# Storing a fill's inputs as high and low parts, so that the wide tiles of the first MLP load both directly

## The chip, the cores and the metric

The kernel runs on one core of one Trainium2 chip. The metric is the time of one execution on the device, in microseconds (us); lower is better. Engines are named as in the profile: PE (matrix multiply), PEld (its weight loads), DVE (vector), ACT (scalar), POOL (GpSimd), SP (the queue from which every DMA of this kernel is issued; the profile writes SPq for its instructions).

## What is computed

Causal attention with a memory term, then two MLPs one after the other, all in float32:

```python
scores = q @ k.T / 8, causal;  a = softmax(scores);  local = a @ v
mem = (phi(q) @ M_prev) / (phi(q) . z_prev + 1e-6)
x0 = gate * mem + (1 - gate) * local      # 4 batches, 8 heads, 576 positions, 64 wide
x  = x0 as 2304 tokens x 512
x1 = elu(x @ w1_in) @ w1_out              # 512 -> 2048 -> 512
out = leaky(x1 @ w2_in) @ w2_out
```

The weights of the MLPs are float64 in memory and are decoded on the chip.

## The kernel before, in words

**Number format.** A matrix product in full precision is made of three products in the faster rounded format (F32R): a value x is split into a high part xh (x rounded, a cast on ACT) and a low part xl (x minus xh, a subtraction on POOL), a weight likewise, and wh·xh, wl·xh and wh·xl are added up in PSUM (`h_mm`, line 615; `o_mm`, line 642). So each x that goes into an MLP costs a cast and a subtraction before PE can use it.

**Order of the work.** First attention, batch by batch. The first MLP is cut in two over its hidden size. The first 7 of its 16 hidden blocks of 128 (NFA, line 47) are worked off as a **fill** between the attention's pieces (`phase1_units`, line 661): each batch is cut into 2 parts of 288 tokens, 8 parts in all (`parts`, line 152). For a part, `u_x` (line 669) gathers its x (one load from `xm_scr` for batch 0; for the other batches two halves from `xq_scr` that DVE adds, line 682), stores it to `x_scr` for later (line 683; batch 0 has it in `xm_scr` already), and splits it into `xh0/xl0` or `xh1/xl1` (`split_x`, line 607: 4 casts on ACT, 4 subtractions on POOL at line 612). `u_h` and `u_o` make the hidden blocks and a partial output, which is copied to a tile `st` and stored to `y_scr` (line 697).

The other 9 hidden blocks follow in the **wide tiles** (line 822): 5 tiles of 512 tokens (the last has 256). A wide tile's x is read back by `load2` (line 814): for each half of 256 tokens, `recut` (line 786) loads the token ranges of the parts into the one staging tile `x` (one buffer, in a pool of its own), then 4 casts on ACT write the high part into `xw0` or `xw1` and 4 subtractions on POOL (line 806) write the low part into `xv0` or `xv1`. Two sets of buffers take turns, so a tile's x is made while the tile before is multiplied. Each hidden block goes through ACT twice (`elu`, lines 631 and 632), DVE twice (line 633, and the cast to `gh` at 244) and POOL once (`gl`, line 626) before `emit_out` multiplies it on. At a tile's end, DVE adds the stored `y` (line 852) half by half, through two buffers `st`, and the sums are stored to `x1_scr` (line 853). The 9 weight blocks of this part are loaded (lines 102, 106) and decoded beside it: ACT 126, DVE 127, 128, 131, ACT 242 (the cast to w), POOL 137 twice. The second MLP then runs in wide tiles of the same kind, and reads its x through `load3` and the same staging tile.

**What sets the order.** The program's order gives each instruction a priority, shifted by `tc.high_priority`, and a scheduler that simulates the engines' time lays every engine's instructions out in one fixed list; each engine, SP among them, then goes through its list in order and waits where it must. The first wide tile's load stands 150 steps ahead of its place (line 820). The load of tile i+1 stands in the program just ahead of the last `emit_out` of tile i (line 845).

**Memory that is shared.** When the fill ends, its pools are closed and new ones take the same memory (`close_mlp`, line 732); a new tile waits for the old tiles under it alone. By the sizes and the order of first use, `xw0` and `xv0` lie on the fill's `x`, `y`, `xh0` and `xl0`; `xw1` on the end of the old `gl`, on both `st` and on `xh1`; `xv1` on `xh1` and `xl1`; the new `e` on the old `e` and the first `gh`.

Of the kernel before, what the change touches and what calls it, by code (L numbers as in the profile page):

```python
# [8 lines left out]
F32 = mybir.dt.float32  # L9
F32R = mybir.dt.float32r  # L10
# [5 lines left out]
P = 128  # L16
# [3 lines left out]
def _f(ap):  # L20
    return ap.bitcast(F32)
# [3 lines left out]
def kernel(  # L25
# [14 lines left out]
    nc = tc.nc  # L40
# [4 lines left out]
    NKC = DM // P  # L45
# [6 lines left out]
    V32 = 1  # L52
# [7 lines left out]
    TN = 256  # L60
    TW = 512
# [9 lines left out]
    dram = ctx.enter_context(tc.tile_pool(name="dram", bufs=1, space=bass.MemoryType.DRAM))  # L71
# [70 lines left out]
    def tile_tok(t):  # L142
        b, ca, cb = t
        r0 = CH[ca][0]
        r1 = CH[cb - 1][0] + CH[cb - 1][1]
        return b * S + r0, r1 - r0

    def halves(n):
        return [(0, n)] if n <= 320 else [(0, n // 2), (n // 2, n // 2)]


    parts = [(i, o, w, tile_tok(t)[0] + o) for i, t in enumerate(tiles1) for o, w in halves(tile_tok(t)[1])]
    xm_scr = [dram.tile([P, NKC, tile_tok(t)[1]], F32, name=f"xm{i}") for i, t in enumerate(tiles1)]
    xq_scr = [
        [dram.tile([P, NKC, tile_tok(t)[1]], F32, name=f"xq{i}_{j}") for j in range(2)] for i, t in enumerate(tiles1)
    ]
    x_scr = [
        xm_scr[t][:, :, o:o + w] if t < V32 else dram.tile([P, NKC, w], F32, name=f"xs{i}")
        for i, (t, o, w, _) in enumerate(parts)
    ]  # L160
    y_scr = [dram.tile([P, NKC, p[2]], F32, name=f"ys{i}") for i, p in enumerate(parts)]
    x1_scr = [dram.tile([P, NKC, TN], F32, name=f"x1s{i}") for i in range(NTT)]

# [43 lines left out]
    def bank(tag):  # L207
        return psum.tile([P, 512], F32, tag=tag, bufs=BANKS[tag], name=tag)
# [31 lines left out]
    def copy(eng, dst, src):  # L240
        if eng == "A":
            nc.scalar.copy(dst, src)  # L242
        else:
            (nc.vector if eng == "V" else nc.gpsimd).tensor_copy(dst, src)  # L244

    def split(hi, lo, src, full=False):
        if full:
            nc.scalar.copy(_f(hi), src)
            return
        nc.scalar.copy(hi, src)  # L250
        nc.vector.tensor_tensor(out=lo, in0=src, in1=_f(hi), op=ALU.subtract)  # L251
# [350 lines left out]
    def mtile(tag, bufs, dt=F32, shape=None):  # L602
        shape = shape or (NW,)
        pool = pools.get(("own", tag), pools["mlp"])
        return pool.tile([P] + list(shape), dt, tag=tag, bufs=bufs, name=tag)

    def split_x(xt, w, par):
        xh = mtile(f"xh{par}", 1, F32R, (NKC, NW))[:, :, 0:w]
        xl = mtile(f"xl{par}", 1, F32R, (NKC, NW))[:, :, 0:w]
        for c in range(NKC):  # L610
            copy(E_XH, xh[:, c], xt[:, c])
            nc.gpsimd.tensor_tensor(out=xl[:, c], in0=xt[:, c], in1=_f(xh[:, c]), op=ALU.subtract)
        return xh, xl

    def h_mm(ph, wi, xh, xl):
        n_mm = 0
        for kc in range(NKC):
            for wj, xx in ((0, xh), (1, xh), (0, xl)):
                nc.tensor.matmul(ph, wi[:, wj, kc, :], xx[:, kc, :], start=n_mm == 0, stop=n_mm == 11)  # L619
                n_mm += 1  # L620
# [8 lines left out]
    def elu(ph, w):  # L629
        e = mtile("e", EB)[:, 0:w]  # L630
        nc.scalar.activation(out=e, in_=ph, func=AF.Relu, scale=-1.0)
        nc.scalar.activation(out=e, in_=e, func=AF.Exp, scale=-1.0)
        nc.vector.scalar_tensor_tensor(out=e, in0=e, scalar=-1.0, in1=ph, op0=ALU.add, op1=ALU.max)  # L633
        return g_split(e, w)
# [7 lines left out]
    def o_mm(py, fs, key, ec, gs, first, last, opens=True, closes=True):  # L642
        for f in fs:
            wo = wo_tiles[key, f]
            gh, gl = gs[f]
            for n_mm, (wj, gg) in enumerate(((0, gh), (1, gh), (0, gl))):
                nc.tensor.matmul(  # L647
                    py, wo[:, wj, ec * P:(ec + 1) * P], gg,
                    start=opens and f == first and n_mm == 0, stop=closes and f == last and n_mm == 2,
                )  # L650
# [5 lines left out]
    def h_bank():  # L656
        nonlocal n_ph
        n_ph += 1
        return bank("tp" if tail and n_ph % 2 else "pm")

    def phase1_units(ti):

        units = []
        for pi, (pt, o, w, _) in enumerate(parts):
            if pt != ti:
                continue
            st = {}

            def u_x(pi=pi, o=o, w=w, st=st):
                xt = mtile("x", 1, F32, (NKC, NW))[:, :, 0:w]  # L670
                if ti < V32:
                    nc.sync.dma_start(xt, xm_scr[ti][:, :, o:o + w])
                    st["x"] = split_x(xt, w, pi % 2)
                    st["g"] = {}
                    return
                x2 = mtile("y", 1, F32, (NKC, NW))[:, :, 0:w]
                for j in range(2):
                    ps, pz = slice(64 * j, 64 * j + 64), slice(64 - 64 * j, 128 - 64 * j)
                    nc.sync.dma_start(xt[ps], xq_scr[ti][j][ps, :, o:o + w])
                    nc.sync.dma_start(x2[ps], xq_scr[ti][j][pz, :, o:o + w])  # L680
                for c in range(NKC):
                    nc.vector.tensor_tensor(out=xt[:, c], in0=xt[:, c], in1=x2[:, c], op=ALU.add)
                nc.sync.dma_start(x_scr[pi], xt)
                st["x"] = split_x(xt, w, pi % 2)
                st["g"] = {}

            def u_h(f, w=w, st=st):
                ph = h_bank()[:, 0:w]
                h_mm(ph, wi_tiles[0, f], *st["x"])
                st["g"][f] = elu(ph, w)  # L690

            def u_o(ec, pi=pi, w=w, st=st):
                py = bank("sc" if tail else "pm")[:, 0:w]
                o_mm(py, range(NFA), 0, ec, st["g"], 0, NFA - 1)
                y = mtile("st", 2)[:, 0:w]
                copy(E_Y, y, py)
                nc.sync.dma_start(y_scr[pi][:, ec], y)

            units.append((0, u_x))
            for f in range(NFA):  # L700
                units.append((HC * 12 * w / 2.4, lambda f=f, u=u_h: u(f)))
            for ec in range(NKC):
                units.append((3 * NFA * w / 2.4, lambda ec=ec, u=u_o: u(ec)))
        return units
# [48 lines left out]
    for c, u, done in att:  # L753
# [11 lines left out]
        while fill and fill[0][0] <= pos and fill[0][1] <= credit:  # L765
            _, c2, u2 = fill.pop(0)
# [19 lines left out]
    def recut(dst, scr, t0, n):  # L786
        for pi, (_, _, w, tok) in enumerate(parts):
            lo, hi = max(tok, t0), min(tok + w, t0 + n)
            if lo < hi:
                nc.sync.dma_start(dst[:, :, lo - t0:hi - t0], scr[pi][:, :, lo - tok:hi - tok])  # L790

    n_wide = 0

    def load_x(fetch, t0, n):

        nonlocal n_wide
        par = n_wide % 2
        n_wide += 1
        xh = mtile(f"xw{par}", 1, F32R, (NKC, TW))[:, :, 0:n]
        xl = mtile(f"xv{par}", 1, F32R, (NKC, TW))[:, :, 0:n]  # L800
        for o in range(0, n, TN):
            xt = mtile("x", 1, F32, (NKC, TN))
            fetch(xt, t0 + o)
            for c in range(NKC):
                copy(E_XH, xh[:, c, o:o + TN], xt[:, c])
                nc.gpsimd.tensor_tensor(  # L806
                    out=xl[:, c, o:o + TN], in0=xt[:, c], in1=_f(xh)[:, c, o:o + TN], op=ALU.subtract
                )
        return xh, xl
# [2 lines left out]
    wide = [(t0, min(TW, NT - t0)) for t0 in range(0, NT, TW)]  # L812

    def load2(t0, n):
        return load_x(lambda xt, t: recut(xt, x_scr, t, TN), t0, n)

    def load3(t0, n):
        return load_x(lambda xt, t: nc.sync.dma_start(xt, x1_scr[t // TN]), t0, n)

    with tc.high_priority(offset=EARLY):  # L820
        cur = load2(*wide[0])
    for gi, (t0, w) in enumerate(wide):
# [21 lines left out]
        if gi + 1 < len(wide):  # L844
            cur = load2(*wide[gi + 1])
# [14 lines left out]
    for gi, (t0, w) in enumerate(wide):  # L860
# [25 lines left out]
        for tb in range(w // P):  # L886
            r0 = t0 + tb * P
            for hf in range(2):
                cs = slice(hf * DM // 2, (hf + 1) * DM // 2)
                o = mtile("st", 2, F32, (DM // 2,))  # L890
# [32 lines left out]
```

## Time and profile before

| what | value |
|---|---|
| median of 3 runs | 1110.76 us (1110.44 to 1112.65) |
| the profiled execution's own time | 1110.38 us |
| its span, first to last instruction | 1108.6 us |
| mean granted clock of PE, as a share of full speed | 0.989 |
| busy: PE | 1062.3 us (96%) |
| busy: PEld | 916.4 us (83%) |
| busy: DVE | 600.1 us (54%) |
| busy: ACT | 493.6 us (45%) |
| busy: POOL | 563.7 us (51%) |
| DMA | 104.43 MB, mean 94 GB/s |

A view by stretches gives each engine's busy time in a stretch, with the granted clock of PE; a timeline lists an engine's instructions in order of time, with the idle time before one in square brackets and the engine or transfer whose end released it; a view of groups sums the instructions of one line. Idle time of an engine other than PE costs nothing by itself. Times in the timelines count from the span's start. Attention and the fill reach to about 470, the first MLP's wide tiles lie at about 453 to 712, and the second MLP is at about 697 to the end.

### The profile page before, as it was taken

Reading aid. Unit: us, or ns where it says so; the run is one execution under the profiler, and the core shown is the slowest. Engines: PE = TensorE matmul, PEld = TensorE weight load, DVE = VectorE, ACT = ScalarE, POOL = GpSimd, SP = SyncE. Lnnn points to the kernel's source line nnn. Section 1 sums busy time; section 2 is a strip of 40 time slices with the busy share of each in tenths; the row PEclk is TensorE's granted clock in tenths of the full one; section 3 lists DMA queues with packets and bytes.
Section 4 is the critical chain, followed back from the end, with each engine's and each line's share of the span. In section 5 each row is a group of like instructions: output and inputs, shape, how many; then the busy total and the mean of one; then the engine's idle time right before and its main releaser. Section 6 shows DMA issues by size and latency. Waiting matters only on the chain.

```text
span 1108.6 us, 17441 instructions
## 1 busy us (share of the span) xinstructions
PE 1062.3 (96%) x5904; PEld 916.4 (83%) x5904; DVE 600.1 (54%) x1398; ACT 493.6 (45%) x1205; POOL 563.7 (51%) x710
## 2 busy tenths in 40 slices
PE   6998899999989998979999999999999999999997
PEld 3877799989979998967777889888888888888896
DVE  6889978787869837656565223655222232132232
ACT  5898878687858635444343223432111111111110
POOL 7676785775747527666575224855322322222222
PEclk9999999999999999989999999999999999999999
DMA  7654533744462147543635113431200100010010
GB/s 180 186 144 96 135 89 92 174 112 116 109 171 80 51 150 225 158 140 124 201 115 168 56 40 96 152 114 38 67 10 1 48 29 1 1 39 1 1 38 20
DMA packets 145912, 104.43 MB, mean 94 GB/s; under 512 B 81440, under 2 KB 139808, under 8 KB 145824
## 3 DMA queue, kind: packets, MB, share of 16 engines
q1 hardware_dynamic: 145824, 103.33, 32.4%
q8 instruction: 47, 0.77, 0.3%
q14 instruction: 41, 0.34, 0.1%
HBM read 73.80 MB, written 25.95 MB: 90 GB/s over the span
## 4 chain that ended last, share of the span: by engine, by line
PE 69%; DMA 8%; DVE 8%; POOL 6%; issue 4%; ACT 3%; SPq 2%; DVEq 0%; POOLq 0%; ACTq 0%
PE pm L619 16%; PE sc L871 14%; PE tp L619 12%; PE sc L647 5%; PE po L871 4%; PE po L525 4%; PE pm L647 4%; PE tp L458 3%; POOL xv L806 2%; PE sc L429 2%; POOL w L137 1%; PE po L647 1%; PE sc L430 1%; DMA wraw<-in_moe_w_out_dram 1%; DMA x1s<-st 1%
## 5 line engine op out<-in xcount | busy, mean ns | idle before, releaser
L626 POOL TENSOR_TENSOR gl<-e,gh 128x512 fp32r<-128x512 f32 (+2 forms) x181 | 202.7, 1123 | 358.3 <-DVE gh L244 314.6
L619 PE MATMUL tp<-xw,w 128*128 128x512 f32 (+1 forms) x504 | 147.1, 374 | 5.6 <-DVE e L633 5.6
L619 PE MATMUL pm<-xw,w 128*128 128x512 f32 (+1 forms) x496 | 143.9, 372 | 0.0
L871 PE MATMUL sc<-w,gh 128*128 128x512 f32 x448 | 137.7, 393 | 0.0
L647 PE MATMUL sc<-gh,w 128*128 128x512 f32 (+2 forms) x438 | 108.6, 347 | 5.7 <-DVE st L852 2.9
L619 PEld LDWEIGHTS tp<-xw,w 128*128 128x128 f32 x504 | 92.2, 190 | 24.3 <-DVE e L633 6.0
L452 POOL TENSOR_SCALAR pt<-pt,rs,omg 128x128 f32<-128x128 f32 (+4 forms) x160 | 102.0, 646 | 19.6 <-DVE rs L447 18.1
L619 PEld LDWEIGHTS pm<-xw,w 128*128 128x128 f32 x496 | 90.5, 188 | 18.4
L437 ACT ACTIVATE pt<-pt,mx 128x128 f32<-128x128 f32 (+4 forms) x160 | 93.3, 584 | 24.9 <-DVE mx L432 23.4
L871 PEld LDWEIGHTS sc<-w,gh 128*128 128x128 f32 x448 | 83.1, 188 | 17.9
L619 PE MATMUL tp<-xv,w 128*128 128x512 f32 (+1 forms) x252 | 94.1, 374 | 0.0
L619 PE MATMUL pm<-xv,w 128*128 128x512 f32 (+1 forms) x248 | 92.0, 371 | 0.0
L647 PEld LDWEIGHTS sc<-gh,w 128*128 128x128 f32 x438 | 75.6, 190 | 17.7 <-issue 3.8
L638 ACT ACTIVATE e<-pm 128x512 f32<-128x512 f32 (+1 forms) x40 | 22.2, 555 | 151.6 <-PE pm L619 151.6
L619 PE MATMUL pm<-xh,w 128*128 128x288 f32 x368 | 82.1, 309 | 5.9 <-DVE e L633 4.5
L244 DVE CAST gh<-e 128x512 fp32r<-128x512 f32 (+2 forms) x146 | 76.2, 524 | 20.6 <-PE po L647 8.0
L458 PE MATMUL tp<-ident,pt 128*128 128x128 f32 x480 | 81.7, 276 | 5.4 <-DVE dl L251 2.0
L871 PE MATMUL sc<-w,gl 128*128 128x512 f32 x224 | 85.4, 393 | 0.0
L639 DVE TENSOR_TENSOR e<-tp,e 128x512 f32<-128x512 f32 (+1 forms) x40 | 25.5, 636 | 107.7 <-ACT e L638 107.6
L639 DVE TENSOR_TENSOR e<-pm,e 128x512 f32<-128x512 f32 (+1 forms) x40 | 25.5, 637 | 106.9 <-ACT e L638 106.9
L137 POOL TENSOR_TENSOR w<-wm,w 128x512 fp32r<-128x512 f32 x50 | 66.2, 1343 | 30.1 <-ACT w L242 30.1
L638 ACT ACTIVATE e<-tp 128x512 f32<-128x512 f32 (+1 forms) x40 | 22.1, 553 | 117.4 <-PE tp L619 117.2
(155 smaller groups left out, 2509.1 us busy)
## 6 DMA issues: line engine op xcount, KB each, us to landing
wraw<-in_moe_w_in_dram SPq DMA_DIRECT2D x32, 512.0 KB, 4.1
wraw<-in_moe_w_out_dram SPq DMA_DIRECT2D x32, 512.0 KB, 4.9
ys<-st SPq DMA_DIRECT2D x32, 144.0 KB, 3.1
x1s<-st SPq DMA_DIRECT2D x36, 128.0 KB, 1.8
x<-x1s SPq DMA_DIRECT2D x9, 512.0 KB, 3.7
out_dram<-st SPq DMA_DIRECT2D x36, 128.0 KB, 1.7
vn<-in_v_dram SPq DMA_DIRECT2D x64, 64.0 KB, 2.4
xq<-xp SPq DMA_DIRECT2D x24, 160.0 KB, 2.0
```

The lines of the kernel that those rows point to most:

```text
L137: nc.gpsimd.tensor_tensor(out=w[:, 1, a], in0=t[:, a], in1=_f(w)[:, 0, a], op=ALU.subtract)
L244: (nc.vector if eng == "V" else nc.gpsimd).tensor_copy(dst, src)
L437: nc.scalar.activation(out=pt[0:m, 0:nk], in_=pt[0:m, 0:nk], func=AF.Exp, scale=-1.0, bias=mx[0:m, last:last + 1], accum_out=self.pd["ss"] ...
L452: nc.gpsimd.tensor_scalar(out=pt, in0=pt, scalar1=rs[0:m, i:i + 1], scalar2=omg[0:m, h:h + 1], op0=ALU.mult, op1=ALU.mult,)
L458: nc.tensor.transpose(dst, self.p[c][:, k0:k0 + kn], ident)
L525: nc.tensor.matmul(po[:, a:b], w, x, start=i == 0, stop=i == len(mms) - 1)
L619: nc.tensor.matmul(ph, wi[:, wj, kc, :], xx[:, kc, :], start=n_mm == 0, stop=n_mm == 11)
L626: nc.gpsimd.tensor_tensor(out=gl, in0=g, in1=_f(gh), op=ALU.subtract)
L638: nc.scalar.mul(t, ph, 0.01)
L639: nc.vector.tensor_tensor(out=t, in0=ph, in1=t, op=ALU.max)
L647: nc.tensor.matmul(py, wo[:, wj, ec * P:(ec + 1) * P], gg, start=opens and f == first and n_mm == 0, stop=closes and f == last and n_mm == 2,)
L871: nc.tensor.matmul(pos[tb], gg[:, tb * P:(tb + 1) * P], wo[:, wj, :], start=f == 0 and n_mm == 0, stop=f == NF - 1 and n_mm == 2,)
```

## The change

The fill stores the high and the low part of each part's x (`xp_scr`, 16 buffers in DRAM) instead of x; for batch 0, which had no store of its own, too. `load2` loads both parts straight into `xw` and `xv`, the whole tile's width at a time, without the staging tile, the casts and the subtractions. `load3` is as it was.

```diff
-    x_scr = [
-        xm_scr[t][:, :, o:o + w] if t < V32 else dram.tile([P, NKC, w], F32, name=f"xs{i}")
-        for i, (t, o, w, _) in enumerate(parts)
-    ]
+    xp_scr = [[dram.tile([P, NKC, p[2]], F32, name=f"x{n}{i}") for i, p in enumerate(parts)] for n in "hl"]
...
             def u_x(pi=pi, o=o, w=w, st=st):
+                def split():
+                    st["x"] = split_x(xt, w, pi % 2)
+                    for n in range(2):
+                        nc.sync.dma_start(xp_scr[n][pi], _f(st["x"][n]))
+                    st["g"] = {}
+
                 xt = mtile("x", 1, F32, (NKC, NW))[:, :, 0:w]
                 if ti < V32:
                     nc.sync.dma_start(xt, xm_scr[ti][:, :, o:o + w])
-                    st["x"] = split_x(xt, w, pi % 2)
-                    st["g"] = {}
+                    split()
                     return
...
-                nc.sync.dma_start(x_scr[pi], xt)
-                st["x"] = split_x(xt, w, pi % 2)
-                st["g"] = {}
+                split()
...
-    def load_x(fetch, t0, n):
-
+    def wide_x():
         nonlocal n_wide
         par = n_wide % 2
         n_wide += 1
-        xh = mtile(f"xw{par}", 1, F32R, (NKC, TW))[:, :, 0:n]
-        xl = mtile(f"xv{par}", 1, F32R, (NKC, TW))[:, :, 0:n]
+        return [mtile(f"{nm}{par}", 1, F32R, (NKC, TW)) for nm in ("xw", "xv")]
+
+    def load_x(fetch, t0, n):
+
+        xh, xl = (x[:, :, 0:n] for x in wide_x())
...
     def load2(t0, n):
-        return load_x(lambda xt, t: recut(xt, x_scr, t, TN), t0, n)
+        xs = wide_x()
+        for x, scr in zip(xs, xp_scr):
+            recut(_f(x), scr, t0, n)
+        return [x[:, :, 0:n] for x in xs]
```

## Rows read from the trace of the kernel before

**Rows 1.** Busy time by stretch: start:end, length, each engine's busy us (instructions), PEclk, DMA.
```profile
428.00:440.00 12.00, 10.14 (x74) 9.67 (x73) 10.36 (x11) 3.71 (x6) 9.95 (x8) 1.00 0.39 140
...
472.00:484.00 12.00, 6.40 (x17) 4.74 (x16) 6.24 (x8) 5.71 (x12) 8.14 (x8) 0.72 0.62 188
...
600.00:700.00 100.00, 100.00 (x520) 84.44 (x519) 30.87 (x62) 29.24 (x60) 36.11 (x37) 1.00 0.22 64
```

**Rows 2.** Timeline of PE: start, us, line, operation, what ended the idle time before it.
```profile
441.83 0.53 PE L647 MATMUL sc<-gh,w 128*128 128x288 f32 x2 [0.86 <-ACT st L242]
...
478.40 1.22 PE L619 MATMUL tp<-xw,w 128*128 128x512 f32 x2 [5.60 <-DVE e L633]
...
483.69 1.67 PE L647 MATMUL sc<-gh,w 128*128 128x512 f32 x6
...
541.61 0.91 PE L647 MATMUL sc<-gh,w 128*128 128x512 f32 x2 [2.37 <-DVE st L852]
...
545.30 0.66 PE L647 MATMUL sc<-gh,w 128*128 128x512 f32 x2
```

**Rows 3.** The chain that ended last, one undisturbed hidden block of a wide tile.
```profile
616.54 2.80 PE tp L619 x12
```

**Rows 4.** Timeline of ACT around 440 and 472.
```profile
440.16 1.33 ACT L242 CAST xw<-x 128x256 fp32r<-128x256 f32 x4 [5.17 <-POOL xl L612]
...
471.05 1.05 ACT L242 CAST w<-wm 128x1024 fp32r<-128x1024 f32 x1 [1.31 <-DVE wm L131]
472.01 0.58 ACT L631 ACTIVATE e<-tp 128x512 f32<-128x512 f32 x1
...
475.77 1.32 ACT L242 CAST xw<-x 128x256 fp32r<-128x256 f32 x4 [2.69 <-DMA ys<-st]
477.00 0.62 ACT L632 ACTIVATE e<-e 128x512 f32<-128x512 f32 x1
477.54 1.12 ACT L126 ACTIVATE wm<-wraw 128x1024 f32<-128x1024 f32 x1
```

**Rows 5.** Timeline of DVE, the same place.
```profile
477.66 0.69 DVE L633 SCALAR_TENSOR_TENSOR e<-e,tp 128x512 f32<-128x512 f32 x1 [6.64 <-ACT e L632]
```

**Rows 6.** Timeline of POOL.
```profile
440.65 2.80 POOL L806 TENSOR_TENSOR xv<-x,xw 128x256 fp32r<-128x256 f32 x4 [0.52 <-ACT xw L242]
...
472.18 2.49 POOL L137 TENSOR_TENSOR w<-wm,w 128x512 fp32r<-128x512 f32 x2 [5.58 <-ACT w L242]
```

**Rows 7.** Matrix products of the first wide tile that read xw, up to the stall.
```profile
452.00:472.80 20.80, 10.21 (x32) 1.00 0.51 152
```

**Rows 8.** Timeline of SP's queue: the first tile's load, the fill's last stores, a tile boundary.
```profile
443.47 1.21 SPq L790 DMA_DIRECT2D x<-xm  x2
...
471.52 0.46 SPq L697 DMA_DIRECT2D ys<-st  x1
...
523.89 1.20 SPq L790 DMA_DIRECT2D x<-xs  x2
...
525.79 0.51 SPq L106 DMA_DIRECT2D wraw<-in_moe_w_out_dram  x1
527.14 8.67 SPq L853 DMA_DIRECT2D x1s<-st  x4
```

**Rows 9.** The stores of x1 (line 853), from issue to landing.
```profile
DMA to landing us min/median/max: 1.7/1.8/5.9
```

**Rows 10.** Groups of the tiles xw, xv and xl: duration min/median/max in ns.
```profile
L242 ACT CAST xw<-x x72: 391/402/409, 440.2 to 961.7; 128x256 fp32r<-128x256 f32 x72
L806 POOL TENSOR_TENSOR xv<-x,xw x72: 722/739/1733, 440.6 to 963.4; 128x256 fp32r<-128x256 f32 x72
L612 POOL TENSOR_TENSOR xl<-x,xh x32: 789/812/1789, 121.4 to 438.3; 128x288 fp32r<-128x288 f32 x32
```

**Rows 11.** DMA issues: count, KB each, median us to landing.
```profile
xs<-x SPq DMA_DIRECT2D x6, 576.0 KB, 3.5
...
x<-x1s SPq DMA_DIRECT2D x9, 512.0 KB, 3.7
```

## The prediction, made before the change was run

> **What bounds the kernel now.** I read the busy time by stretches first, to see where PE rests. Inside the first MLP's wide tiles it does not: from 600 to 700 it is busy for 100 of 100 us at full clock [rows 1]. There the casts, the subtractions and the staging tile are hidden, and taking them away is worth nothing. What is left to gain lies where the fill ends and the wide tiles begin: from 428 to 440 PE is busy for 10.14 of 12 us, from 472 to 484 for 6.40 of 12, and in the latter the granted clock is 0.72 [rows 1]. The timeline of PE then gives the single waits: 0.86 us at 441.83 for ACT, 5.60 us at 478.40 for DVE, and 2.37 us at 541.61 for DVE's additions at the end of the first wide tile [rows 2].
>
> The large one is followed back through the timelines. PE waits at 478.40 for DVE's step of line 633 at 477.66 [rows 5], which waited 6.64 us for ACT's second step (line 632) at 477.00. ACT had done the first step (line 631) at 472.01, so this second step could have followed within a microsecond or so. But ACT goes through its list in order, and between them stand four casts to xw for the second wide tile, which sat until 475.77 and ended what they waited for with the landing of the last store of y from st [rows 4, 8]. The reason is in the code: xw1 lies on the fill's st. The casts' data is not needed for tens of microseconds; their wait for the buffer blocks work that PE needs at once. The same happens at 440.16, where four casts to xw0 hold ACT for 5.17 us until the last part's subtraction has read x [rows 4], and PE's 0.86 us is for a copy of ACT behind them.
>
> After its long rest PE also runs slowly: the 12 products from 478.40 to 483.69 take 5.29 us where an undisturbed block takes 2.80 [rows 2, 3], 2.5 us lost. At 541.61 the 9 products up to 545.30 take 3.69 us, against 2.10 (9/12 of 2.80), 1.6 us lost [rows 2, 3].
>
> **The change, part by part.**
>
> Removed from the wide tiles: 36 of the 72 casts to xw, at 0.40 us 14.5 us of ACT, and 36 of the 72 subtractions to xv, at 0.74 us 26.6 us of POOL [rows 10]. As engine time this is worth nothing where PE is full. What counts is the two places where the casts block.
>
> At 472: without the casts ACT goes from line 631 to line 632 at about 473.1 (two first steps of 0.58 us from 472.01), not 477.00. That alone starts PE 3.9 us sooner, at 474.5, with 1.7 us of rest left. POOL loses four subtractions of 2.80 us at 440.65 and four more at 450 [rows 6], both ahead of the weight chain whose cast at 471.05 stands ahead of ACT's step at 472.01 [rows 4]; that chain should run 2 to 4 us earlier, which takes most of the rest away too. I take 5.0 of the 5.60 us and the 2.5 us of slow clock: **-7.5**. Bounds: -3.9, if the weight chain is no earlier and the short rest still slows the clock, and -8.1, all of it.
>
> At 441: the 0.86 us goes with the casts: **-0.9**. Bounds 0 and -2.7, the latter with the 1.86 us that PE rests between 428 and 440 [rows 1], because x is also free for the next part without waiting for its store (3.5 us to land, rows 11).
>
> At 541: the additions of the first wide tile wait for their two buffers st, whose stores take 5.9 us to land at worst where the median is 1.8 [rows 9]. Ahead of those stores at 527.14 stood 1 MB of x, issued at 523.89, and weights at 525.79 [rows 8]. After the change the next tile's x no longer passes through one staging tile; it can leave as soon as PE has read xw0 for the last time, at about 514 (the casts that needed xw0 ran at about 517), and should be over before the stores begin. The weights stay. Bounds 0 and -4.0 (2.37 + 1.6); I take **-1.5**, nearer to zero since two of the three transfers stay.
>
> Added in the fill: 16 stores of 576 KB in place of 6, which land in about 3.5 us and which nobody waits for soon [rows 11]. Their cost is in SP's queue: the store of the low part waits for POOL's four subtractions, which run 4 x 0.81 = 3.2 us behind the casts [rows 10], and behind it in SP's list are the attention's loads of q, k and v, the copies of kk and the stores of xq. At worst 8 x 3.2 = 26 us of SP would be lost, of which PE would see little, since those loads are issued well ahead. The scheduler puts a store where it thinks it ready, so a wait is the difference between its model and the chip. I take **+1.0**, between -1 (x is free sooner, and 6 stores of x are gone) and +7.
>
> Added for the first wide tile: its x was partly in the staging tile before the fill's buffers came free; now 2 MB in 4 loads can leave only at about 440.1, behind the last part's stores. Half a MB takes 3.7 us [rows 11], so the four quarters take at most 14.8 us one after the other, and the tile would be there between 448 and 455, where the old way has it after four more casts behind the load at 443.47 [rows 8]: about 454. What covers a delay: by 472.8 PE had done 32 of the xw products [rows 7] and half as many with xv, 48 or four blocks, 11.2 us at 2.80; the other 8 us or so of that stretch are the fill's, and can go ahead of them. **+0.5**, between 0 and +4.
>
> For the other tiles, 24 loads in place of 16, each tile's 2 MB 20 us or more ahead of its use: nothing, but for the second rival. The sum is -7.5 - 0.9 - 1.5 + 1.0 + 0.5 = **-8.4 us**. The profiled execution took 1110.38 us, so 1102.0; the median of the runs stands 0.4 above it: **1102.4 us**.
>
> **The rivals.**
>
> *The wait only changes hands.* When the casts are gone, the next instruction in ACT's list may be line 126 of the weight decoding, at 477.54 now [rows 4]. It needs POOL's subtractions of the weights, which end at 472.18 + 2.49 = 474.7 [rows 6]. Placed ahead of line 632 it would run from 474.7 to 475.8, and PE would start at 477.3: 1.2 us won, the clock low as before, and the 1.5 us of added costs against it. That gives about 1110.5. For it: the scheduler mixes the two chains everywhere. Against it: line 632 stands ahead of line 126 now.
>
> *SP's queue takes the wait over, slower than before.* First the row: what ACT waited for at 440.16 and 475.77 was memory to come free, and that need stays [rows 4]. The Trainium skill, "DMA: Bandwidth & Descriptors", section "Anatomy of one DMA", states that a DMA's semaphore wait is done by the issuing sequencer before dispatch; by that rule the wait for xw moves from ACT to SP and holds all DMAs behind it. No row here prices it for these loads. As a mechanism of this kernel: at each of the four boundaries between wide tiles, 2 MB stand in SP's list ahead of the y loads and the x1 stores. If they leave late, those stores land in 5.9 us or more at every boundary [rows 9], and each costs PE what the first costs now, 2.37 + 1.6 = 4.0 us. Three more of them are +12.0, and the -1.5 falls away: -7.5 - 0.9 + 1.5 + 12.0 = +5.1, that is 1115.9 us. It decides at about 520, 7 us (2 MB at twice the rate of a single load) ahead of the stores at 527.14: earlier, it costs nothing. For it: one such case is in the trace. Against it: PE is done with the old buffer some 13 us before the stores.
>
> A whole new list for every engine comes with any change here, and the attention before 428 can shift by a few us either way; that widens the range, and I have no row that says which way.
>
> **How the numbers follow.** Chances: the forecast 0.65, the wait that changes hands 0.15, SP's queue 0.20. The forecast's own range is 1097 to 1107 (its bounds of -15 and of about -3, cut where several would have to come together). The range for 8 in 10 is 1097 to 1114: it takes in the first rival and reaches most of the way to the second. A measurement of this kernel can tell about 0.2% from no change, 2.2 us. Faster by more than that: the forecast nearly whole and a little of the rest, 0.66. Within it: 0.13. Slower: 0.21.
>
> **What would show each step.** Right: in the changed profile PE's wait of over 5 us around 472 is gone and the clock of that stretch is near 1.00; ACT's line 632 follows line 631 within 2 us there; no cast to xw before the second MLP; PE's wait for ACT's copy near 441 is gone. At the first boundary the stores of line 853 land in clearly less than 5.9 us. Wrong: PE waits for xw or xv loads at the start of the first wide tile; waits of 2 us for line 852 at several boundaries; longer waits of SP for line 612 with PE waiting for kk or k in the attention; or the same rest at 472 with line 126 or the weight cast in the casts' place.

## The result, and the profile after

The changed kernel took **1098.55 us** (median of 4 runs, 1095.36 to 1102.78), the kernel before 1111.43 us in the runs beside it: a ratio of 0.989, 95% interval 0.9858 to 0.9922, that is 12.9 us less. Timed again with the last experiments it was 1097.81 us against 1111.06 (0.9902, 0.9876 to 0.9927). The forecast was 1102.4 us in a range of 1097 to 1114. Sign and place were right; the gain is one and a half times the 8.4 us of the sum, and its cause, as the experiments show, was told only in part.

The profiled execution took 1098.26 us with a span of 1096.2. First the total busy times of the changed kernel (engine, busy us, share of the span, instructions):

```profile
PE 1057.6 (96%) x5904; PEld 912.7 (83%) x5904; DVE 600.3 (55%) x1398; ACT 484.8 (44%) x1169; POOL 530.6 (48%) x674
```

PE does the same products as before. To see where the 12.4 us of span went, two marks at equal work serve: the attention's last product `po<-dl,vv` and the first MLP's last product `sc<-gl`. In the view of a line, the last two times of a row are the starts of its first and of its last product. Before:

```profile
L525 PE MATMUL po<-dl,vv x96: 276/280/373, 104.6 to 402.5; 128*128 128x256 f32 x96
...
L647 PE MATMUL sc<-gl,w x219: 276/303/628, 382.4 to 706.8; 128*128 128x512 f32 x54, 128*128 128x288 f32 x42, 128*128 128x256 f32 x14
```

After (all lines behind 157 are renumbered: 647 is now 644, 619 is 616, 631 to 633 are 628 to 630, 852 and 853 are 857 and 858, 612 is 609):

```profile
L522 PE MATMUL po<-dl,vv x96: 276/280/415, 104.4 to 404.1; 128*128 128x256 f32 x96
...
L644 PE MATMUL sc<-gl,w x219: 276/298/499, 384.5 to 694.3; 128*128 128x512 f32 x54, 128*128 128x288 f32 x42, 128*128 128x256 f32 x14
```

Up to the first mark the changed kernel is 1.6 us later. Between the marks it needs 290.2 us instead of 304.3: 14.1 us less. From the second mark to the end of the span both need the same, 401.8 and 401.9 us. So the whole gain lies between the end of the attention and the end of the first MLP, as the prediction said, and ahead of it the changed kernel is a little later.

The busy times by stretch of the changed kernel (columns as in [rows 1]; the five busy times are those of PE, PEld, DVE, ACT and POOL):

```profile
428.00:440.00 12.00, 11.57 (x86) 11.11 (x85) 8.78 (x13) 4.67 (x10) 9.32 (x10) 1.00 0.70 215
...
472.00:484.00 12.00, 11.07 (x48) 8.65 (x47) 9.53 (x12) 5.71 (x7) 6.97 (x5) 1.00 0.93 288
536.00:548.00 12.00, 12.00 (x53) 9.66 (x52) 6.40 (x9) 3.08 (x4) 4.96 (x4) 1.00 0.67 215
600.00:700.00 100.00, 99.55 (x535) 84.80 (x533) 35.71 (x68) 31.44 (x63) 40.03 (x40) 1.00 0.27 82
```

From 472 to 484 PE is busy for 11.07 us where it was 6.40, at a granted clock of 1.00 where it was 0.72 [rows 1]. The stretch with the first tile boundary, 536 to 548, has no rest at all; before, it read:

```profile
536.00:548.00 12.00, 9.63 (x35) 7.35 (x35) 6.19 (x12) 3.41 (x4) 3.73 (x3) 0.86 0.70 210
```

From 600 to 700, where PE was full before, nothing was to be had and nothing came. The timeline of PE in the changed kernel (start, us, what ended the idle time before) shows what remains of the waits:

```profile
421.64 0.54 PE L616 MATMUL tp<-xh,w 128*128 128x288 f32 x2 [1.07 <-DVE e L630]
...
473.30 0.73 PE L616 MATMUL tp<-xw,w 128*128 128x512 f32 x2 [0.93 <-DVE e L630]
```

The 5.60 us of [rows 2] are now 0.93, for the same step of DVE. The timeline of ACT shows why:

```profile
468.26 1.14 ACT L126 ACTIVATE wm<-wraw 128x1024 f32<-128x1024 f32 x1 [2.65 <-POOL w L137]
...
469.58 0.61 ACT L628 ACTIVATE e<-tp 128x512 f32<-128x512 f32 x1
...
470.55 1.17 ACT L629 ACTIVATE e<-e 128x512 f32<-128x512 f32 x2
```

Line 629 (the old 632) runs 0.97 us after line 628 (the old 631); before, 5 us and four casts lay between them [rows 4]. Ahead of both stands line 126, the weight decoding, and it waits for POOL's line 137. That line becomes important below.

At the first tile boundary the timeline of SP's queue in the changed kernel reads:

```profile
511.67 1.88 SPq L790 DMA_DIRECT2D xw<-xh  x3
513.59 4.38 SPq L790 DMA_DIRECT2D xv<-xl  x3
...
523.17 5.54 SPq L858 DMA_DIRECT2D x1s<-st  x4
```

The next tile's loads leave 11.5 us ahead of the first four x1 stores, where before 3.3 us lay between them [rows 8]. From issue to landing those four stores took, in the changed kernel from 520 to 530:

```profile
DMA to landing us min/median/max: 1.8/2.3/2.8
```

and in the kernel before, from 524 to 537:

```profile
DMA to landing us min/median/max: 1.7/3.8/5.9
```

What the new stores do to SP is seen in the fill. The waits of SP's queue from 0 to 430 us in the changed kernel (who waited for whom: us in total, times, longest) hold nine rows for the new stores, line 670, of 15.3 us in all. The five largest:

```profile
SPq L670 <- ACT e L628: 4.4, 1, 4.4
...
SPq L670 <- ACT xh L239: 3.2, 1, 3.2
...
SPq L670 <- ACT e L629: 2.2, 1, 2.2
...
SPq L670 <- ACT kk L298: 1.9, 1, 1.9
...
SPq L670 <- POOL xl L609: 1.7, 2, 1.5
```

### The profile page after: what moved, and what is told of

Its sections match the earlier page's. It is cut to its first block, busy times and chain, and to the rows that moved or that the text cites. A ratio compares the mean times of both kernels' runs of the same rounds, so it can differ in the third digit from the quotient of the medians.

```text
span 1096.2 us, 17406 instructions
## 1 busy us (share of the span) xinstructions
PE 1057.6 (96%) x5904; PEld 912.7 (83%) x5904; DVE 600.3 (55%) x1398; ACT 484.8 (44%) x1169; POOL 530.6 (48%) x674
## 4 chain that ended last, share of the span: by engine, by line
PE 73%; DMA 8%; DVE 7%; POOL 3%; ACT 3%; SPq 3%; issue 3%; DVEq 0%; POOLq 0%; ACTq 0%
PE pm L616 17%; PE sc L876 14%; PE tp L616 13%; PE sc L644 8%; PE po L876 4%; PE pm L644 4%; PE po L522 3%; PE tp L455 3%; PE po L644 2%; DMA wraw<-in_moe_w_out_dram 2%; DMA x<-xq 2%; SPq L212 2%; PE sc L426 1%; PE sc L427 1%; PE pm L522 1%
## 5 line engine op out<-in xcount | busy, mean ns | idle before, releaser
L623 POOL TENSOR_TENSOR gl<-e,gh 128x512 fp32r<-128x512 f32 (+2 forms) x181 | 199.8, 1108 | 369.8 <-DVE gh L241 291.9
L644 PE MATMUL sc<-gh,w 128*128 128x512 f32 (+2 forms) x438 | 106.0, 343 | 1.1 <-DVE st L857 0.7
L429 DVE CUSTOM_DVE_ANT_0 pt<-sc,mask 128x128 f32<-128x128 f32 (+4 forms) x160 | 69.4, 446 | 8.6 <-PE sc L427 4.3
```

Of the source, the lines that this page charges most:

```text
L429: nc.vector.tensor_tensor_reduce(out=pt[0:m, k0:k0 + n], in0=sc[0:m, 0:n], in1=mk, op0=ALU.add, op1=ALU.min, scale=-0.125, scalar=mx[0:m, ...
L623: nc.gpsimd.tensor_tensor(out=gl, in0=g, in1=_f(gh), op=ALU.subtract)
L644: nc.tensor.matmul(py, wo[:, wj, ec * P:(ec + 1) * P], gg, start=opens and f == first and n_mm == 0, stop=closes and f == last and n_mm == 2,)
```

## The experiments

Gains below are against the kernel before in runs on the same chip. In the diffs the lines of the kernel that an experiment starts from are those of the changed kernel, unless "before" is said. Two questions are put: which part of the removed work or waits gave the 12.9 us, and what the new stores cost.

**Half of the work back: the casts, or the subtractions.** The first kernel loads the high part through the staging tile and casts it again, the low part directly:

```diff
-        xs = wide_x()
-        for x, scr in zip(xs, xp_scr):
-            recut(_f(x), scr, t0, n)
+        xh, xl = wide_x()
+        recut(_f(xl), xp_scr[1], t0, n)
+        for o in range(0, n, TN):
+            xt = mtile("x", 1, F32, (NKC, TN))
+            recut(xt, xp_scr[0], t0 + o, TN)
+            for c in range(NKC):
+                copy(E_XH, xh[:, c, o:o + TN], xt[:, c])
```

> The changed kernel with the casts alone put back: the wide tiles of the first MLP load the low part directly, but the high part through the staging tile and 36 casts on ACT. Theory (ACT's casts, waiting for a buffer, held back line 629, the second step of elu, at 472): the rest of PE at 472 is back with 4 to 6 us and a low clock after it, and the staging tile may bring back the wait at the first tile boundary; the time is 6 to 11 us above the changed kernel, 1105 to 1110 us. Rival (the 36 subtractions on POOL stood in the way of the weight decoding and of gl, and the casts were harmless): within 2 us of the changed kernel, 1097 to 1101 us, no rest over 2 us at 472.

The second does the same to the low part, with 36 subtractions of a tile of zeros on POOL and no casts:

```diff
+                nc.gpsimd.tensor_tensor(out=xl[:, c, o:o + TN], in0=xt[:, c], in1=zero, op=ALU.subtract)
```

> The changed kernel with POOL's work alone put back: the high part is loaded directly, the low part through the staging tile and 36 subtractions (of a tile of zeros) on POOL. Theory (ACT's casts): no rest over 2.5 us at 472, within 3 us of the changed kernel, 1097 to 1102 us. Rival (POOL's subtractions): 6 us or more above it, 1105 to 1110 us.

With the casts it took 1103.71 us (ratio 0.9925, 0.9894 to 0.9956), with the subtractions 1103.46 us (0.9922, 0.9892 to 0.9951). Against the kernel before (1110.74 us) they keep 7.0 and 7.3 us of the 12.9: by the medians each half gives back between 5 and 6, and neither is the whole. The intervals of these ratios overlap with the changed kernel's, so the sizes are rough. Both times lie between what the two sides of each expectation said, and settle neither. The casts missed what was expected of them: they do wait again for st at 475, for 0.99 us, but the rest of PE at 472 does not come back. PE's longest wait from 440 to 600 is elsewhere, in the timeline of PE in the kernel with the casts:

```profile
450.11 0.58 PE L644 MATMUL sc<-gh,w 128*128 128x288 f32 x2 [1.74 <-ACT st L239]
```

It is the wait that stood at 441 before, and longer: in ACT's list the casts to xw sit again until the fill's last subtraction has read x, and the copy to st stands behind them (timeline of ACT):

```profile
446.59 1.33 ACT L239 CAST xw<-x 128x256 fp32r<-128x256 f32 x4 [5.24 <-POOL xl L609]
```

In the kernel with the subtractions a rest is at its old place, shorter, in the timeline of PE:

```profile
477.38 0.74 PE L616 MATMUL tp<-xw,w 128*128 128x512 f32 x2 [2.15 <-DVE e L630]
```

and here no cast can be its cause, for there is none. The timeline of ACT has the weight cast between the two steps, waiting for the decoding:

```profile
475.03 1.05 ACT L239 CAST w<-wm 128x1024 fp32r<-128x1024 f32 x1 [2.01 <-DVE wm L131]
475.98 1.15 ACT L629 ACTIVATE e<-e 128x512 f32<-128x512 f32 x2
```

So PE's rest can come by way of the weight decoding alone, with no buffer waited for by a cast. Between the two marks the kernel with the casts needs 294.4 us and the one with the subtractions 301.3, against 290.2 and 304.3 above. That looks like the larger share for the subtractions, but it is one execution each, and the latter was the slowest of its six.

**The wait away, the work kept.** Two kernels leave the kernel before as it is and only place the wide tiles differently in memory: in their traces every engine has the same instructions in the same order as before. In the first, the order in which xw and xv get their memory is swapped, so that xv1 and not xw1 lies on the fill's st:

```diff
-        xh = mtile(f"xw{par}", 1, F32R, (NKC, TW))[:, :, 0:n]
         xl = mtile(f"xv{par}", 1, F32R, (NKC, TW))[:, :, 0:n]
+        xh = mtile(f"xw{par}", 1, F32R, (NKC, TW))[:, :, 0:n]
```

> The kernel before with nothing taken away: only the order in which xw and xv get their memory is swapped, so that xv1 and no longer xw1 lies on the fill's st, and xv0 on x. The casts keep their place and their 0.40 us each, but no longer wait for the last store of y; POOL's subtractions do. Theory (it is the casts' waiting, not their work, that cost the time): no cast to xw waits for a store from st at 472, the rest of PE there shrinks from 5.6 to under 3 us, and the time is 3 to 8 us below the kernel before, 1103 to 1108 us. Rival (the casts' own 14.5 us on ACT, or the work on POOL): within 2 us of the kernel before, 1109 to 1113 us.

The second allocates xw1 and xv1 before the first wide tile, so that neither lies on st:

```diff
+    for nm in ("xw1", "xv1"):
+        mtile(nm, 1, F32R, (NKC, TW))
     with tc.high_priority(offset=EARLY):
         cur = load2(*wide[0])
```

> The kernel before with nothing taken away: xw1 and xv1 get their memory first, so that both lie on the fill's e and gh (free when the fill's last product has run, at about 468.6) and no longer on st (free when its last store has landed, at about 474.7). The attention's lists stay as they were. Theory (what cost the time is a wait for that store in a queue that goes in order, ACT's before, POOL's when the two were swapped): no cast to xw and no subtraction waits for a store of y at 472, PE's rest there falls from 5.6 us to under 2.5 without a new wait for gl, and the time is 4 to 8 us below the kernel before, 1103 to 1107 us. Rival (as with the swap, another wait takes its place, and the work itself must go): within 2 us of the kernel before.

The swap took 1111.4 us (0.9999, 0.9975 to 1.0024), the earlier allocation 1110.04 us (0.9993, 0.9973 to 1.0013): no gain from either, where 3 to 8 and 4 to 8 us were expected; the rival held both times. And yet the wait that the prediction put first is gone. In the swapped kernel the casts follow line 631 at once (timeline of ACT):

```profile
472.30 1.32 ACT L242 CAST xw<-x 128x256 fp32r<-128x256 f32 x4
473.51 0.64 ACT L632 ACTIVATE e<-e 128x512 f32<-128x512 f32 x1
```

and PE's rest is 2.86 us instead of 5.60. Then POOL is late with what PE needs next. The timeline of POOL in the swapped kernel:

```profile
475.05 4.70 POOL L806 TENSOR_TENSOR xv<-x,xw 128x256 fp32r<-128x256 f32 x4 [1.04 <-DMA ys<-st]
479.71 3.52 POOL L626 TENSOR_TENSOR gl<-e,gh 128x512 fp32r<-128x512 f32 x2
```

and in its timeline of PE the new waits for gl:

```profile
474.92 0.73 PE L619 MATMUL tp<-xw,w 128*128 128x512 f32 x2 [2.86 <-DVE e L633]
...
489.77 0.96 PE L647 MATMUL sc<-gl,w 128*128 128x512 f32 x3 [2.35 <-POOL gl L626]
```

From 400 to 720 us PE waits 6.5 us for gl there, in the kernel before 1.4, and its waits in that stretch add up to 15.0 us against 13.3. In the kernel with the earlier allocation no buffer is waited for at that place at all, and still POOL does its four subtractions ahead of gl. Its timelines of POOL and of PE:

```profile
475.99 3.45 POOL L806 TENSOR_TENSOR xv<-x,xw 128x256 fp32r<-128x256 f32 x4
479.40 2.32 POOL L626 TENSOR_TENSOR gl<-e,gh 128x512 fp32r<-128x512 f32 x1
```

```profile
476.94 0.74 PE L619 MATMUL tp<-xw,w 128*128 128x512 f32 x2 [2.79 <-DVE e L633]
...
540.74 1.19 PE L647 MATMUL sc<-gh,w 128*128 128x512 f32 x2 [2.32 <-DVE st L854]
```

PE's waits from 400 to 720 add up to 13.3 us here, as before, and between the marks both kernels need 303.8 us against 304.3. Taking the wait away without the work is worth nothing that can be measured: the time appears as waits for gl and at the tile boundary.

**The work back, the buffers free.** The reverse: the changed kernel with all 36 casts and 36 subtractions as ballast. They read the loaded xw and xv and write a staging tile that nobody uses, so the result does not depend on them.

```diff
+        for o in range(0, n, TN):
+            xt = mtile("x", 1, F32, (NKC, TN)).bitcast(F32R)
+            for c in range(NKC):
+                copy(E_XH, xt[:, c], _f(xs[0])[:, c, o:o + TN])
+                nc.gpsimd.tensor_tensor(
+                    out=xt[:, c], in0=_f(xs[1])[:, c, o:o + TN], in1=_f(xs[0])[:, c, o:o + TN], op=ALU.subtract
+                )
```

> The changed kernel with the old work of ACT and POOL kept as ballast: after the loads into xw and xv, 36 casts and 36 subtractions of the same shapes read them and write the staging tile, and nobody uses the result. PE's data no longer passes through them, and they wait for no buffer that the fill still holds, only for the loads. Theory A (what cost the time is that the casts and subtractions stand in ACT's and POOL's lists and wait there for the fill's memory): within 3 us of the changed kernel, 1097 to 1102 us. Theory B (their work on two engines that are also decoding weights and making e, gh and gl, 28.8 of 30 us of POOL from 430 to 460, is what costs): 6 us or more above it, 1105 to 1112 us, with PE waiting for gl and for line 630.

It took 1106.63 us (0.9961, 0.9943 to 0.9979): 8.8 us more by the medians than the changed kernel beside it, and 6.6 by the ratios, whose intervals do not overlap. Between the marks it needs 300.0 us. The rest of PE at 472 is back (timeline of PE):

```profile
477.28 1.22 PE L616 MATMUL tp<-xw,w 128*128 128x512 f32 x2 [4.66 <-DVE e L630]
```

How it comes back can be followed. In the timeline of POOL four ballast subtractions run ahead of a pair of line 137, the weight decoding:

```profile
453.96 5.32 POOL L824 TENSOR_TENSOR x<-xv,xw 128x256 fp32r<-128x256 f32 x4
459.24 2.38 POOL L623 TENSOR_TENSOR gl<-e,gh 128x288 fp32r<-128x288 f32 x3
461.58 2.53 POOL L137 TENSOR_TENSOR w<-wm,w 128x512 fp32r<-128x512 f32 x2
469.69 2.54 POOL L137 TENSOR_TENSOR w<-wm,w 128x512 fp32r<-128x512 f32 x2 [5.57 <-ACT w L239]
```

In the changed kernel the pairs are at other times (its timeline of POOL):

```profile
457.58 2.54 POOL L137 TENSOR_TENSOR w<-wm,w 128x512 fp32r<-128x512 f32 x2
465.69 2.54 POOL L137 TENSOR_TENSOR w<-wm,w 128x512 fp32r<-128x512 f32 x2 [5.57 <-ACT w L239]
```

Both pairs are 4.0 us later with the ballast. And 4.0 us later is ACT's line 126, which waits for them, and by that the steps of the hidden blocks behind it, in the timeline of ACT of the kernel with the ballast:

```profile
472.26 1.12 ACT L126 ACTIVATE wm<-wraw 128x1024 f32<-128x1024 f32 x1 [2.20 <-POOL w L137]
473.28 0.59 ACT L628 ACTIVATE e<-tp 128x512 f32<-128x512 f32 x1
```

against 468.26 and 469.58 above; PE's rest is 3.7 us longer (4.66 against 0.93). No wide buffer is waited for in this chain. It is the queue of work in POOL's list, handed on by ACT's list. POOL's share of the stretch from 428 to 460 (columns as in [rows 1], POOL's busy us the fifth) points the same way: before

```profile
428.00:460.00 32.00, 28.96 (x196) 26.98 (x195) 23.17 (x30) 16.92 (x36) 28.76 (x27) 1.00 0.53 170
```

with the change

```profile
428.00:460.00 32.00, 31.57 (x230) 30.78 (x229) 21.43 (x32) 15.06 (x30) 20.93 (x21) 1.00 0.69 232
```

POOL was busy for 28.76 of 32 us where its work decides, and is for 20.93; with the ballast it is 24.60, so the busy time alone does not tell how long PE will rest. Two limits: some of the ballast on ACT also waits for the loads it reads (8.8 us in all) and for its staging tile (5.9), and the engines' lists differ from those of the changed kernel once the ballast begins. So the 8.8 us is not the price of the work alone.

**The stores alone, the loads alone.** The kernel before with the 16 new stores added and read by nobody, its six stores of x kept:

```diff
+                for n in range(2):
+                    nc.sync.dma_start(xp_scr[n][pi], _f(st["x"][n]))
```

> The kernel before with 16 stores of the high and low parts added in the fill (the store of x stays, nothing reads the new ones): the cost of the fill's side by itself. Theory (SP's queue waits a little for POOL's subtractions): 0 to 3 us above the kernel before, 1111 to 1114 us; the attention's last product (line 525) starts about 1.5 us later than the 402.3 of before, as in the changed kernel. Rival (the stores cost nothing and the shift of 1.5 us in the changed kernel is another list order): within 1 us of before, the last product within 0.5 us of 402.3. Second rival (SP's queue is a bottleneck in the attention): 5 us or more above.

The other way round: the wide tiles load without staging, but the fill stores x alone, as before. Both parts are then loaded from x, so the low part is x itself and not what the cast leaves; the amount of work is the changed kernel's without its stores. Its output leaves out the split and is not the MLP's; only its time is of use.

```diff
-        for x, scr in zip(xs, xp_scr):
-            recut(_f(x), scr, t0, n)
+        for x in xs:
+            recut(_f(x), x_scr, t0, n)
```

> The change's loads without its stores: the fill stores x as before, and the wide tiles of the first MLP load xw and xv both from that x, without staging tile, casts and subtractions (the low part is then x itself and not x minus the high part; the transfers are of the same size). The attention's lists stay those of before. Theory (the loads bring the gain of 12 to 13 us, and the stores cost the 1.5 us by which the changed kernel's attention ended later): 1.5 to 3 us below the changed kernel, 1095 to 1098 us. Rival (the stores cost the 6.8 us that they cost beside the old loads): 1090 to 1094 us. Second rival (the gain is in the other list of the attention and the fill): above 1104 us.

The stores alone cost 6.8 us (1117.5 us; 1.0055, 1.0033 to 1.0077), with six stores more than the change has; 0 to 3 were expected. Its attention ends at 407.5, 5.0 us later than before and not 1.5, and between the marks it needs 306.8 us, 2.5 more, with a longer rest of PE:

```profile
485.05 1.22 PE L620 MATMUL tp<-xw,w 128*128 128x512 f32 x2 [8.92 <-DVE e L634]
```

The loads alone gain 17.0 us by the medians (1094.0 us; 0.9855, 0.9832 to 0.9879), at the edge of what the rival said. Against the 12.9 and 13.2 of the whole change that makes about 4 us for the store side: 1094.0 against 1098.55 and 1097.81. In the timeline of PE of the kernel with the loads alone two waits of over a microsecond are left between 404 and 600:

```profile
417.27 0.53 PE L619 MATMUL tp<-xh,w 128*128 128x288 f32 x2 [1.68 <-DVE e L633]
...
468.72 0.73 PE L619 MATMUL tp<-xw,w 128*128 128x512 f32 x2 [1.70 <-DVE e L633]
```

Its marks are 400.1 and 688.9. From the end of the attention on it needs 288.8 us, about as long as the changed kernel (290.2 and, timed again, 289.6). What else it saves is ahead of the first mark, and not all of that is the stores': it ends the attention 2.4 us earlier than the kernel before, with the same lists up to there. The attention's end in the four profiled kernels that have the old stores and the same list up to there is 400.1, 401.7, 402.5 and 402.5 us; in the five with the new ones it is 403.5, 404.0, 404.1, 404.6 and 409.2. The cost, 2 us by the middle of these and 4 by the times, lies in the attention. That it is the stores' own is not shown: from 133 us on, where the first of them stands, they bring a new list for every engine, and in the two kernels with another list, below, the attention ends at 406.0 and 408.0, 3.5 and 3.9 us later, with the same stores.

**Is it the waits of SP's queue there?** The changed kernel with the two stores three hidden blocks later in the program, when their data has long been there:

```diff
-                    for n in range(2):
-                        nc.sync.dma_start(xp_scr[n][pi], _f(st["x"][n]))
...
+                if f == 3:
+                    for n in range(2):
+                        nc.sync.dma_start(xp_scr[n][pi], _f(st["x"][n]))
```

> The changed kernel with the fill's stores of the two parts moved: each part's two stores stand three hidden blocks later in the program, when the subtractions are surely done. Theory (the loads alone gave 1094.0 us and the stores cost 4 to 5 us because SP's queue waits for ACT and POOL ahead of them, 11.7 us in all in the trace of the changed kernel): 2 to 4 us below the changed kernel, 1094 to 1097 us, and SP's waits ahead of these stores under 3 us. Rival (the stores cost by their traffic): within 1.5 us of the changed kernel.

> The changed kernel once more, so that it and the two others are timed on one chip: 1096 to 1101 us by its 4 runs.

The late stores took 1095.97 us (0.9883, 0.9859 to 0.9907), the changed kernel beside them 1097.81 (0.9902, 0.9876 to 0.9927). The intervals overlap, so a gain of 1.8 us is not shown. SP still waits ahead of the late stores, though less: 8.6 us in seven rows, where under 3 were expected and the changed kernel has 15.3 (the expectation's 11.7 are its four largest rows). The waits of SP's queue, 0 to 430 us, of the kernel with late stores, the two largest rows:

```profile
SPq L688 <- ACT xh L239: 4.0, 2, 3.5
...
SPq L688 <- POOL xl L609: 2.2, 2, 1.8
```

The attention ended at 404.3, no earlier. And in the kernel with the stores alone, which lost the most, SP waits only 4.5 us ahead of them up to 430. So the sum of these waits does not go with the cost. Whether the stores cost by SP's waits, by the memory traffic or by the new list stays open. It is the fastest version with the right values that was run.

**Is it luck of the lists?** The scheduler makes a new list for every change. So both kernels were also run with another of its settings, which gives every engine another list:

```diff
-    PC = 200
+    PC = 210
```

> The kernel before with another order of work: the planner's cost of a preparation step in the attention is 210 in place of 200 (line 55), which changes where the fill's pieces fall, and nothing else. It shows how much of a time is the luck of a list. Theory (the rest at 472 comes from the wait for the buffer, whatever the list): PE again rests for 3 us or more at the start of the wide tiles, and the time is within 5 us of the kernel before, 1106 to 1116 us. Rival (the rest at 472 is an accident of one list): no rest over 2 us there, 1100 to 1105 us.

> The changed kernel with the same other order of work, 210 in place of 200. Theory: 8 to 16 us below the kernel before with that order, no rest over 2 us where the wide tiles start. Rival (list luck made a good part of the 12.9 us): less than 6 us below it.

The kernel before took 1116.41 us so, the changed one 1100.40: 16.0 us apart. The same rest is in the one and not in the other. Timeline of PE, before with the other list:

```profile
485.17 1.22 PE L619 MATMUL tp<-xw,w 128*128 128x512 f32 x2 [5.47 <-DVE e L633]
```

and the changed kernel with the other list:

```profile
476.83 0.73 PE L616 MATMUL tp<-xw,w 128*128 128x512 f32 x2 [0.71 <-DVE e L630]
```

The gain belongs to the change, under both lists. The list alone moves the changed kernel by about 2 us and the kernel before by 5.5, a little more than the 5 expected.

## Why the prediction was right, and where it was off

**What bounds the kernel.** Right: the stage that got faster is the one named, and the full stretch behind it gave nothing.

**The 472 term, -7.5.** Measured -7.2: a wait of 5.60 us became 0.93 and the slow clock behind it (2.5 us) went. Its size was right, its cause only half. The prediction put the casts' wait for st first and the earlier weight chain second, as what "takes most of the rest away too". The swap and the earlier allocation show that the first alone leaves 2.8 us of rest and turns the remainder into waits for gl; the ballast shows the second to be enough to bring back 4.66 us. Within the limits of the ballast named above, it is the work in POOL's and ACT's lists beside the weight decoding, and the buffer wait on top of it. How the casts and the subtractions divide it isn't settled: either half alone gave back 5 to 6 us, with intervals of some 3 us to each side.

**The 441 term, -0.9.** The wait for ACT's copy is gone. In the stretch from 428 to 440 PE also gained 1.4 us (10.14 to 11.57), which was in the bound of 2.7 and not in the sum. Against it stands a new wait of 1.07 us at 421.64.

**The boundary term, -1.5.** This was undersized. The wait of 2.37 us and the slow 1.6 behind it are both gone, -4.0, the whole of the bound. "Two of the three transfers stay" weighed the wrong thing, and misread the first of them: the two loads of x at 523.89 carry 320 and 192 KB, not 1 MB. The load of x did leave early, at 511.67, as the prediction said from 514, and the four stores then landed within 2.8 us instead of 5.9. That the landing is what PE's additions waited for is argued from these rows; no run took it alone. Small waits from 550 to 600 that no term counted, 0.90 and 0.58 us, went too: in the changed kernel PE rests for less than half a microsecond between 490 and 600. With these, and the new wait against them, the measured terms add up to 13.9 of the 14.1 us between the marks.

**The stores, +1.0.** Undersized as well: 2 to 4 us, by the attention's end and by the times (17.0 for the loads alone, 12.9 and 13.2 for the whole), within the bounds of -1 and +7. "PE would see little" was too hopeful if this is the stores' doing; the new list, for which the prediction widened its range by "a few us either way" before 428, is the other candidate. The wait that the prediction described, for POOL's subtractions ahead of the store of the low part, came to 1.7 us up to 430 and not to 26 at worst; most of SP's 15.3 us is for ACT.

**The first tile's load, +0.5.** Nothing. The loads left at 436.03 and not 440.1, and by 472.8 PE had done 32 of the xw products with them, as before [rows 7].

Together the load side was taken at -7.5 - 0.9 - 1.5 + 0.5 = -9.4 and measured -14.1 between the marks (-15.5 in the kernel with the loads alone, -17.0 by its median); the store side was taken at +1.0 and measured +2 to +4. The two errors lay on opposite sides, and by that luck the forecast time came within 4 us.

**The rivals.** The wait did not change hands in the changed kernel: line 126 stands ahead of line 628 there, early enough. In the kernel with the subtractions it did, with the weight cast between lines 628 and 629. SP's queue did not take the wait over at the boundaries. It did wait for PE to be done with an old buffer, as this row of the waits of SP's queue from 500 to 700 in the changed kernel shows:

```profile
SPq L790 <- PE tp L616: 19.9, 1, 19.9
```

but PE has no wait of half a microsecond behind it up to the second mark, and at the first boundary the loads left at 511.67, ahead of the point of 520 that was to decide. The Trainium skill, "DMA: Bandwidth & Descriptors", section "Anatomy of one DMA" (written there for the path of gpsimd), has it that the semaphore wait is done by the issuing sequencer; the 19.9 us here and the 15.3 us in the fill agree for SP. The 19.9 us cost PE nothing that shows, and whether the waits in the fill cost anything is left open.

**The numbers.** The time fell on the side that had 0.66 and inside the range; one result does not test a chance. The forecast's own bound of -15 (its terms' far ends add up to -15.8) was "cut where several would have to come together"; several did. The first rival's 1110.5 is 1111.1 by its own terms (1110.8 - 1.2 + 1.5), which changes nothing.

## What to carry to other kernels

Where a full engine rests at a change of phase, look for all that stands in the lists of the helper engines around the chain it waits for, and not only for the instruction that blocks: removing that one wait moved the time to the next late result, removing the work gained about 1%. Price new stores by a run with them alone: here the waits of the queue ahead of them did not tell their cost. And run both kernels with another instruction order, since the order alone moves a kernel by several microseconds.

## What the runs showed that was not expected

The same program does not repeat to 0.2% here: the kernel before gave 1105.8 to 1116.7 us over 22 runs beside the first experiments, with the middle steady at 1110.7 to 1111.4 in all the rounds. In single profiles of the kernels with the changed one's list up to there, the attention ended at 403.5 to 409.2 us, so a difference of a few microseconds in that stage between two profiles is no finding by itself.

A rest of PE that was shortened did not always bring time: from 5.60 us to 2.86 and 2.79 in the two kernels with other memory, the total stayed within 0.1%.
